# Joining a gated product to the seven block products of an output stage (Trainium2, one core)

## The chip, the cores and the metric

The kernel runs on one NeuronCore of one Trainium2 chip. The metric is device time in microseconds (us) of one execution. The kernel before takes 266.28 us (median of 4 runs, 266.19 to 266.54). PE is TensorE, PEld its weight loads, DVE is VectorE, ACT is ScalarE, POOL is GpSimd, SP the engine that issues the DMAs.

## The reference, cut to what matters

```python
xn = layernorm(x)                                    # x: 2048 x 640
# branch A: a diagonal complex recurrence over the 2048 steps, then the output map
h[t] = Lam_bar * h[t-1] + xn[t] @ B_bar.T            # 640 complex states
yA   = 2 * (h @ C.T).real + xn * Dskip               # re and im of h against re and im of C: K = 2 x 640
# branch B: a gated MLP with a mixing over time
z  = gelu(xn @ w_in)                                 # 2048 x 1728
g  = w_sp @ layernorm(z[:, 864:]) + b_sp[:, None]    # "spatial" product, 2048 x 2048 x 864
yB = (z[:, :864] * g) @ w_out                        # K = 864
out = x + yA + yB                                    # 2048 x 640
```

So the output is one sum over h (K = 1280, ten k-tiles of 128) and over the gated features (K = 864, six k-tiles of 128 and one of 96).

## The kernel before: what the change and the argument touch

The kernel lists all its operations with the data they read and write, and a scheduler of its own, with estimated durations, puts them in a fixed order on each engine. TensorE's order is the program's order. At run time each engine goes through its list in order and waits on semaphores. An operation that waits therefore holds up everything behind it on its engine.

The output is made in eight "pairs" of two row tiles. For each pair, a 2 x 2 x 2 block product of h and C is done with seven block products instead of eight (Winograd's form); each has five k-tiles. VectorE makes the sums that this form needs: those of C once (`ct_comb`), those of h for each pair (`h_comb`). The gated part is added without that form: four groups of seven k-tiles (`og`).

```python
# ... out_pair(j), cut: A, B are blocks, S, T are sums of blocks
prods = dict(P1=(A(0, 0), B(0, 0)), P2=(A(1, 0), B(1, 0)), P3=(S(3), B(1, 1)), P4=(A(1, 1), T(2)),
             P5=(S(0), B(0, 1)), P6=(S(1), T(0)), P7=(S(2), T(1)))
# prod: for q in range(5): e.matmul(ps[:, bk, c0:c1], lf(q), rf(q)[:, c0:c1], ...)    5 matmuls of 320 columns
# og:   for k in range(7): e.matmul(ps[:, bk, c0:c1], gv[0:kk, k, :], wov[0:kk, k, ...])  7 of them
X = bk()
prod("P1", X, True)
Z = bk()
cp(Z, X, "p1")                     # ScalarE copies PSUM bank X to Z; X goes on accumulating
while later:
    later.pop()()                  # the c22 group of the pair before
Q = bk()
prod("P5", Q, True)
add(fv(t12), Q, bv(0, 1), "t12"); add(fv(t22), Q, bv(1, 1), "t22")      # VectorE
prod("P6", X, False)               # must wait for the copy of X
V = bk()
cp(V, X, "u2")
prod("P2", Z, False);  og(0, 0, Z, False);  add(ov(0, 0), Z, bv(0, 0), "c11b")
prod("P7", X, False)
W = bk()                           # ... ScalarE copies X to W ("u3"); in the last pair in two parts, W and W2
prod("P3", V, False);  og(0, 1, V, False);  add(ov(0, 1), V, fv(t12), "c12b");  store(0)
prod("P4", X, False);  og(1, 0, X, False);  add(ov(1, 0), X, bv(1, 0), "c21b")
# finish(): og(1, 1, W), add "c22b", store(1): put off to the next pair; in the last pair done at once, in two parts
```

Before that comes the spatial stage, in the same form: eight rounds of seven products of eight k-tiles of 432 columns.

```python
prod(X, "A11", "B11", True, "P1")
ev(f(p1), X, b0, p1.iv(), "p1_%d" % j)               # ScalarE: PSUM to f32 in SBUF, with a bias
# ... P5, P6
prod(Z, "A12", "B21", True, "P2")
dve(tt(half(c0, 0), pb(Z), f(p1), ALU.add), ...)     # VectorE: c11 = P1 + P2
```

Two more parts matter. The "fixes" bring the recurrence's carried state into h: for each pair but the last, ScalarE scales it into one of four buffers `pq_m` (70 operations in all), and VectorE adds the buffer to h. And there are small VectorE operations on a few numbers per partition: 16 for powers of the eigenvalues, and the statistics of the second LayerNorm in four groups of four tiles.

## Time and profile before

| | before |
|---|---|
| time, median | 266.28 us |
| PE busy, matmuls | 258.7 us of a span of 263.9, 1517 |
| DVE busy | 238.8 us |
| ACT busy | 174.5 us |
| output stage, first matmul to last VectorE add | 69.12 us (192.44 to 261.56) |

The page's first part gives the busy time of each engine, its share of the span and its instructions:

```profile
PE 258.7 (98%) x1517; PEld 154.4 (58%) x1521; DVE 238.8 (91%) x574; ACT 174.5 (66%) x315; POOL 24.0 (9%) x41
```

Two engines look full. The chain that ended last says which one matters; its shares of the span by engine, then the costliest groups:

```profile
PE 95%; DMA 1%; SPq 1%; DVE 1%; issue 0%; POOL 0%
...
L994 PE MATMUL ps<-arena 128*128 128x432 bf16 x448 | 82.2, 346 | 0.0
...
L1113 PE MATMUL ps<-arena 128*128 128x320 bf16 x280 | 43.1, 299 | 0.0
```

L994 is the spatial stage, L1113 the h products; the gated groups are L1125. The 299 ns are one matmul from start to end; they overlap. What a matmul costs in a stream is read from the chain in order of time (start, us, what). This is one output period, from a P5 on (the first line is P5, P6 and P2); the last line is cut short by the end of the window:

```profile
201.86 2.04 PE ps L1113 x15
203.90 0.95 PE ps L1125 x7
204.85 1.36 PE ps L1113 x10
206.21 0.95 PE ps L1125 x7
207.16 0.68 PE ps L1113 x5
207.84 0.95 PE ps L1125 x7
208.79 0.68 PE ps L1113 x5
209.48 0.54 PE ps L1125 x4
```

Fifteen matmuls of 320 columns take 2.04 us, 0.136 each, and each piece begins where the one before ends: there is no gap. From the P1 of one pair to that of the next are 63 matmuls, 8.57 us. A change that takes matmuls away here should gain 0.136 us for each, as long as nothing else stops PE.

The first matmuls of the output stage and the end of the kernel, as timelines of PE and of VectorE in order of time (start, us, engine, line; idle time before and its releaser in brackets):

```profile
192.44 2.88 PE L1113 MATMUL ps<-arena 128*128 128x320 bf16 x20
...
258.45 0.84 PE L1113 MATMUL ps<-arena 128*128 128x320 bf16 x5
259.13 2.09 PE L1125 MATMUL ps<-arena 128*128 128x320 bf16 x21
...
260.28 0.49 DVE L1140 TENSOR_TENSOR arena<-ps,arena 128x320 bf16<-128x320 f32 x1 [1.14 <-PE ps L1125]
260.87 0.69 DVE L1187 TENSOR_TENSOR arena<-ps,arena 128x192 bf16<-128x192 f32 x2
```

The c21 add (260.28) runs while PE still does the 14 short matmuls of c22. The last add ends at 261.56, 0.34 us after PE.

### The profile page before, as it was taken

How to read it: one execution, taken by the hardware profiler on the slowest of the kernel's cores; microseconds unless marked ns; L12 is line 12 of the kernel's file. 1: busy time of each engine (PE TensorE's matmuls, PEld its weight loads, DVE VectorE, ACT ScalarE, POOL GpSimd, SP SyncE). 2: the span in 40 equal slices, each digit the busy share in tenths (PEclk: the TensorE clock that was granted, in tenths of full speed). 3: DMA queues.
4: the chain of work that ended last, by engine and by line, in shares of the span. 5: the costliest groups of instructions: out<-in, count | busy, mean ns of one | idle time of the engine just before them, and what ended most of it. 6: DMA issues, size and time to landing. Idle time of an engine off the chain costs nothing.

```text
span 263.9 us, 4352 instructions
## 1 busy us (share of the span) xinstructions
PE 258.7 (98%) x1517; PEld 154.4 (58%) x1521; DVE 238.8 (91%) x574; ACT 174.5 (66%) x315; POOL 24.0 (9%) x41
## 2 busy tenths in 40 slices
PE   7999999999999999999999999999999999999995
PEld 2555554444446777755555555555567777777774
DVE  4999999999999999999999999999999999965332
ACT  4899999989967454432223564689999999711110
POOL 4255076300000000000000000000000000000000
PEclk9999999999999999999999999999999999999999
DMA  6966999995002766498888978997245456675411
GB/s 201 361 83 125 195 221 197 301 234 104 0 0 58 202 186 170 125 234 154 213 201 156 225 139 192 192 250 225 52 137 142 113 126 156 147 214 132 99 52 50
DMA packets 88243, 41.98 MB, mean 159 GB/s; under 512 B 70974, under 2 KB 88222, under 8 KB 88222
## 3 DMA queue, kind: packets, MB, share of 16 engines
q1 hardware_dynamic: 88078, 41.66, 65.9%
q8 instruction: 12, 0.20, 0.3%
q14 instruction: 9, 0.07, 0.1%
q10 hardware_dynamic: 144, 0.05, 0.1%
HBM read 12.27 MB, written 12.45 MB: 94 GB/s over the span
## 4 chain that ended last, share of the span: by engine, by line
PE 95%; DMA 1%; SPq 1%; DVE 1%; issue 0%; POOL 0%
PE ps L994 31%; PE ps L596 19%; PE ps L679 16%; PE ps L1113 14%; PE ps L1125 12%; PE ps L617 2%; DMA arena<-in_A_x_dram 1%; SPq L370 1%; PE ps L560 0%; POOL arena L539 0%; DVE arena L544 0%; DVE arena L534 0%; DVE arena L1187 0%; DVE arena L537 0%; DVE arena L525 0%
## 5 line engine op out<-in xcount | busy, mean ns | idle before, releaser
L994 PE MATMUL ps<-arena 128*128 128x432 bf16 x448 | 82.2, 346 | 0.0
L994 PEld LDWEIGHTS ps<-arena 128*128 128x128 bf16 x448 | 43.7, 98 | 38.3 <-ACT arena L1007 0.8
L596 PE MATMUL ps<-arena 128*128 128x432 bf16 x280 | 51.6, 346 | 0.0
L786 ACT ACTIVATE arena<-arena 128x512 bf16<-128x512 bf16 x70 | 45.2, 712 | 1.7 <-DVE arena L751 1.4
L596 PEld LDWEIGHTS ps<-arena 128*128 128x128 bf16 x280 | 34.7, 124 | 16.1
L679 PE MATMUL ps<-arena 128*128 128x512 bf16 x196 | 43.0, 379 | 0.2
L1113 PE MATMUL ps<-arena 128*128 128x320 bf16 x280 | 43.1, 299 | 0.0
L1007 ACT ACTIVATE arena<-ps,arena 128x432 f32<-128x432 f32 (+1 forms) x32 | 19.6, 615 | 29.9 <-PE ps L994 29.9
L1125 PE MATMUL ps<-arena 128*128 128x320 bf16 (+3 forms) x231 | 35.6, 295 | 0.0
L1113 PEld LDWEIGHTS ps<-arena 128*128 128x128 bf16 x280 | 27.2, 97 | 11.0 <-ACT ps L1148 0.2
L679 PEld LDWEIGHTS ps<-arena 128*128 128x128 bf16 x200 | 19.6, 98 | 23.5 <-DMA arena<-in_A_B_im_dram 0.2
L1140 DVE TENSOR_TENSOR arena<-ps,arena 128x320 bf16<-128x320 f32 (+1 forms) x40 | 18.6, 484 | 12.5 <-PE ps L1125 11.9
L1125 PEld LDWEIGHTS ps<-arena 128*128 128x128 bf16 (+1 forms) x231 | 22.3, 98 | 8.3
L709 DVE SCALAR_TENSOR_TENSOR arena<-arena 128x512 f32<-128x512 bf16 x35 | 25.5, 744 | 0.0
L685 ACT CAST arena<-ps 128x512 bf16<-128x512 f32 x40 | 21.3, 601 | 4.4 <-PE ps L679 4.3
L790 DVE TENSOR_TENSOR arena<-arena 128x1024 bf16<-128x1024 bf16 (+1 forms) x42 | 23.6, 593 | 0.0
L665 ACT ACTIVATE arena<-ps 128x864 bf16<-128x864 f32 x16 | 14.3, 891 | 13.5 <-PE ps L596 13.4
L951 DVE TENSOR_TENSOR arena<-arena 128x1024 bf16<-128x1024 bf16 x32 | 21.3, 684 | 0.6 <-DMA arena<-in_B_w_sp_dram 0.6
L731 DVE TENSOR_TENSOR arena<-arena 128x512 f32<-128x512 f32 (+2 forms) x40 | 21.4, 550 | 0.0
L1148 ACT COPY ps<-ps 128x320 f32<-128x320 f32 x16 | 6.6, 412 | 16.6 <-PE ps L1113 16.6
L714 DVE SCALAR_TENSOR_TENSOR arena<-arena 128x256 bf16<-128x256 bf16 (+1 forms) x35 | 16.6, 477 | 0.0
L711 DVE SCALAR_TENSOR_TENSOR arena<-arena 128x256 bf16<-128x256 bf16 (+1 forms) x35 | 16.6, 475 | 0.0
(103 smaller groups left out, 259.4 us busy)
## 6 DMA issues: line engine op xcount, KB each, us to landing
g_scratch<-arena SPq DMA_DIRECT2D x16, 224.0 KB, 3.0
z_scratch<-arena SPq DMA_DIRECT2D x16, 216.0 KB, 2.5
arena<-z_scratch SPq DMA_DIRECT2D x8, 432.0 KB, 5.0
arena<-in_A_x_dram SPq DMA_DIRECT2D x16, 160.0 KB, 4.0
base_scratch<-arena SPq DMA_DIRECT2D x16, 160.0 KB, 2.2
arena<-base_scratch SPq DMA_DIRECT2D x16, 160.0 KB, 2.5
out_dram<-arena SPq DMA_DIRECT2D x15, 160.0 KB, 2.4
arena<-in_B_w_in_dram SPq DMA_DIRECT2D x6, 216.0 KB, 3.7
```

The lines of the kernel that those rows point to most:

```text
L596: r = e.matmul(ps[:, b + h, 0:FG], lhs(k), winv[:, k, hcol * FH + h * FG:hcol * FH + (h + 1) * FG], start=(k == 0), stop=(k == ND - 1))
L679: r = e.matmul(ps[:, b + ri, :], btv[:, ri, k, q * 128:(q + 1) * 128], xnTv[:, k, tq * 512:(tq + 1) * 512], start=(k == 0), stop=(k == ND ...
L685: act(lambda e, ri=ri: e.copy(o[:, ri, tq], ps[:, b + ri, :].rearrange("p (m j) -> p j m", j=8)), [bank(b + ri)], [l_m.iv((q * 8 + j) * 10 ...
L709: dve(lambda e: e.scalar_tensor_tensor(tv, prev, lr, cur, op0=ALU.mult, op1=ALU.add), pr + [l_iv(q, j)] + cr, [t.iv()], cd(512) + PTR, nm ...
L731: tt = lambda o, a, b, op: (lambda e: e.tensor_tensor(o, a, b, op))
L786: act(lambda e, pv=pv, hv=hv, lo=lo, sc=sc: e.activation(pv, hv[:, lo:lo + 2, 1:257], ACT.Identity, scale=sc), [h.iv(), Civ(cn)], [m.iv((q ...
L790: dve(lambda e, mv=mv, lq=lq: e.tensor_tensor(lq, lq, mv, ALU.add), li + [m.iv(0, 1024 * n)], li, cd(512 * n, 2), "fix%s%d%d" % (nm, q0, j))
L951: dve(lambda e: e.tensor_tensor(o.ap(1024), x.ap(1024), y.ap(1024), op), [x.iv(), y.iv()], [o.iv()], cd(1024, 2), "%s_%d" % (name, j))
L994: r = e.matmul(ps[:, bk, 0:FG], lv_[:, k, :], rv[k], start=(first and k == 0), stop=(k == 7), skip_group_check=True)
L1007: act(lambda e: e.activation(o, pb(bk), ACT.Identity, bias=bias), [bank(bk)] + bi, [dst], ca(FG, psum=True, ptr=1), name)
L1113: r = e.matmul(ps[:, bk, c0:c1], lf(q), rf(q)[:, c0:c1], start=(first and q == 0), stop=(q == 4), skip_group_check=True)
L1125: r = e.matmul(ps[:, bk, c0:c1], gv[0:kk, k, :], wov[0:kk, k, n * HD + c0:n * HD + c1], start=(first and k == 0), stop=(k == 6), skip_grou ...
```

## The change

Its intent: the gated product is another part of the same sum over K, so six of its k-tiles can join the block form: three k-tiles to each of the two K halves. Then the seven products have eight k-tiles each, and only the 96-row remainder is left for `og`. Four groups of six (24 matmuls) become seven groups of three (21): three fewer a pair. (In all it is 30 fewer and not 24, because the last c22 group was done in two parts, as 14 short matmuls, and is now 2; in columns it is 24 times 320.) VectorE must make the sums for the gated tiles too. To give it room, c11 is summed in PSUM: ScalarE copies P1 from one bank to another, PE adds P2 to it, and ScalarE evicts the sum with the bias. And the small VectorE operations become fewer.

```diff
-        pq_m = [q1.sub(2048) for _ in range(3)]          # and a fourth further down: four fix buffers
+        pq_m = [q2.sub(2048) for _ in range(3)]          # three
-        cb_m: 3 buffers, g_m: 4                           (cut)
+        cb_m: 2 buffers, g_m: 2, and wt_m: 3 for the sums of w_out
@@ small operations (cut)
-            for k in range(1, 9):                         # 16 operations on 5 numbers each
-                ... tensor_scalar(C("kr")[:, sl], C("dl")[:, 0:5], float(k), ...)
-                ... tensor_scalar(C("an")[:, ...], C("dl")[:, 5:10], float(k), ...)
+            pool(iota C("kv"))                            # then 2 operations on 40 numbers
+            dve(tensor_tensor(k3(C("kr")), k3(C("kv")), kb(C("dl")[:, 0:5]), ALU.mult))
+            dve(tensor_tensor(k3(C("an")[:, 40:80]), k3(C("kv")), kb(C("dl")[:, 5:10]), ALU.mult))
-            if i % 4 == 3:
-                z2_norm(i - 3, i + 1)
+            if i % 8 == 7:
+                z2_norm(i - 7, i + 1)
@@ c11
-            ev(f(p1), X, b0, p1.iv(), "p1_%d" % j)
+            act(lambda e: e.copy(pb(Z), pb(X)), [bank(X)], [bank(Z)], ...)
-            prod(Z, "A12", "B21", True, "P2")
-            dve(tt(half(c0, 0), pb(Z), f(p1), ALU.add), ...)
+            prod(Z, "A12", "B21", False, "P2")
+            ev(half(c0, 0), Z, b0, hiv(c0, 0), "c11_%d" % j)
@@ the join
+        def g_comb(j):                                    # four sums of 384 bf16 per pair, as in h_comb
+            ...
+            tt(S1, a21, a22, ALU.add, gi, i1, "GS1")
+            tt(S2, S1, a11, ALU.subtract, gi + [i1], i2, "GS2")
+            tt(S3, a11, a21, ALU.subtract, gi, i3, "GS3")
+            tt(S4, a12, S2, ALU.subtract, gi + [i2], i4, "GS4")
-                    for q in range(5):
+                    for q in range(8):                    # prod: k-tiles 5 to 7 are gated ones
-                    for k in range(7):                    # og
+                e.matmul(ps[:, bk, c0:c1], gvs[h][0:96, 6, :], wov[0:96, 6, ...], start=False, ...)   # og: one
-            while later:
-                later.pop()()
-                later.append(finish)
+                finish()                                  # c22 no longer put off
```

That a matmul may add to what ScalarE wrote rests on PSUM's accumulation. The Trainium skill, "PSUM — Partial Sum Buffer" (section "The four PSUM rules"), says that a matmul without the first-of-group flag adds to the old data where a matmul has written since the bank was last cleared by that flag, whoever wrote the data. The output stage used the same trick before.

More of the change, by code (lines that the diff above doesn't have):

```diff
@@ L298, in bass_parallel_sum__ssm_conv_s5__mixer_gmlp__prompt_kernel @@
         q1 = r1.again()
-        pq_m = [q1.sub(2048) for _ in range(3)]
+        wo_m = q1.sub(7 * 1280)
         cf_m = [q1.sub(1728) for _ in range(5)]
-        cb_m = [q1.sub(1728) for _ in range(3)]
+        cb_m = [q1.sub(1728) for _ in range(2)]
         z1i_m = [q1.sub(3456) for _ in range(2)]
-        g_m = [q1.sub(1792) for _ in range(4)]
+        g_m = [q1.sub(1792) for _ in range(2)]
         ct4_m = q1.sub(3200)
+        wt_m = [q1.sub(1920)]
         cp_m = Mem(r1.lo + 37760, 12800)
@@ L307, in bass_parallel_sum__ssm_conv_s5__mixer_gmlp__prompt_kernel @@
         q2 = r2.again()
-        wo_m = q2.sub(7 * 1280)
+        pq_m = [q2.sub(2048) for _ in range(3)]
         gT_m = [q2.sub(1792) for _ in range(4)]
         ct_m = [q2.sub(3200) for _ in range(2)] + [ct4_m]
-        pq_m.append(q2.sub(2048))
+        wt_m += [q2.sub(1920) for _ in range(2)]
         q3 = r3.again()
@@ L325, in bass_parallel_sum__ssm_conv_s5__mixer_gmlp__prompt_kernel @@
         prm_m = cst(128, BF16)
-        c_m = cst(440)
+        c_m = cst(512)
         st_m = cst(NT * 16)
@@ L409, in C @@
                 o = sum(c for _, c in cpos.values())
-                assert (o + n) <= 440
+                assert (o + n) <= 512
                 cpos[name] = (o, n)
@@ L476, in bass_parallel_sum__ssm_conv_s5__mixer_gmlp__prompt_kernel @@
              [ident_m.iv()], [ident_m.iv()], 0.3, "id1")
-        C("half", 4)
+        C("half", 8)
         C("e", 40)
@@ L634, in z2_norm @@
             if t0 < NHALF:
-                dve(lambda e: e.tensor_tensor(v(0), v(0), v(7), ALU.add), [vi(0), vi(7)], [vi(0)], 0.08, "z2s" + n)
+                h0, h7 = st2v[:, 0, t0:NHALF], st2v[:, 7, t0:NHALF]
+                dve(lambda e: e.tensor_tensor(h0, h0, h7, ALU.add), [s2iv(0, t0, NHALF), s2iv(7, t0, NHALF)],
+                    [s2iv(0, t0, NHALF)], 0.08, "z2s" + n)
             dve(lambda e: e.tensor_scalar(v(2), v(0), 1.0 / FH, None, op0=ALU.mult), [vi(0)], [vi(2)], 0.08, "z2m" + n)
@@ L814, in s5_consts @@
             C("an", 80)
-            for k in range(1, 9):
-                sl = slice((k - 1) * 5, k * 5)
-                dve(lambda e, k=k, sl=sl: e.tensor_scalar(C("kr")[:, sl], C("dl")[:, 0:5], float(k), None, op0=ALU.mult),
-                    [Civ("dl")], [Civ("kr")], 0.07, "kr%d" % k)
-                dve(lambda e, k=k, sl=sl: e.tensor_scalar(C("an")[:, 40 + (k - 1) * 5:40 + k * 5], C("dl")[:, 5:10],
-                                                          float(k), None, op0=ALU.mult),
-                    [Civ("dl")], [Civ("an")], 0.07, "an%d" % k)
+            C("kv", 40)
+            pool(lambda e: e.iota(C("kv"), pattern=[[1, 8], [0, 5]], base=1, channel_multiplier=0,
+                                  allow_small_or_imprecise_dtypes=True), [], [Civ("kv")], 0.2, "kv")
+            k3 = lambda a: a.rearrange("p (k q) -> p k q", k=8)
+            kb = lambda a: a.rearrange("p (o q) -> p o q", o=1).broadcast_to([128, 8, 5])
+            dve(lambda e: e.tensor_tensor(k3(C("kr")), k3(C("kv")), kb(C("dl")[:, 0:5]), ALU.mult), [Civ("dl"), Civ("kv")],
+                [Civ("kr")], 0.11, "kr")
+            dve(lambda e: e.tensor_tensor(k3(C("an")[:, 40:80]), k3(C("kv")), kb(C("dl")[:, 5:10]), ALU.mult),
+                [Civ("dl"), Civ("kv")], [Civ("an")], 0.11, "an")
             pool(lambda e: e.tensor_tensor(C("rk"), C("e"), C("kr"), ALU.pow), [Civ("kr"), Civ("e")], [Civ("rk")],
@@ L1008, in ev @@
                         ca(FG, psum=True, ptr=1), name)
-            p1, p5, u2, u3 = [ring(cf_m, ncf) for _ in range(4)]
+            p5, u2, u3 = [ring(cf_m, ncf) for _ in range(3)]
             f = lambda m: m.ap(FG, FP32)
@@ L1015, in spatial @@
             prod(X, "A11", "B11", True, "P1")
-            ev(f(p1), X, b0, p1.iv(), "p1_%d" % j)
+            act(lambda e: e.copy(pb(Z), pb(X)), [bank(X)], [bank(Z)], ca(FG, psum=True), "p1_%d" % j)
             prod(Y, "S1", "T1", True, "P5")
@@ L1020, in spatial @@
             ev(f(u2), X, b0, u2.iv(), "u2_%d" % j)
-            prod(Z, "A12", "B21", True, "P2")
-            dve(tt(half(c0, 0), pb(Z), f(p1), ALU.add), [bank(Z), p1.iv()], [hiv(c0, 0)], cd(FG), "c11_%d" % j)
+            prod(Z, "A12", "B21", False, "P2")
+            ev(half(c0, 0), Z, b0, hiv(c0, 0), "c11_%d" % j)
             prod(X, "S3", "T3", False, "P7")
@@ L1031, in spatial @@
             for h, c in ((0, c0), (1, c1)):
-                gm = g_m[ng[0] % 4]
-                gsem = ng[0] % 4
+                gm = g_m[ng[0] % 2]
                 ng[0] += 1
@@ L1041, in gate_st @@
             n = 2 * j + h
-            gsem = n % 4
+            gsem = n % 2
             dma("sp", g_d[n], gm.ap(896), [gm.iv()], [("gd", n, n + 1)], 128 * 1792, "gst%d%d" % (j, h), sem="gst%d" % gsem)
@@ L1058, in bass_parallel_sum__ssm_conv_s5__mixer_gmlp__prompt_kernel @@
         ctv = [m.ap(ND * HD).rearrange("p (q n) -> p q n", q=ND) for m in ct_m]
-        def ct_comb():
-            b11, b12 = cpv[:, 0, :, 0:HD], cpv[:, 0, :, HD:D]
-            b21, b22 = cpv[:, 1, :, 0:HD], cpv[:, 1, :, HD:D]
-            ci = [cp_m.iv()]
-            t2, t3, t4 = ctv
-            for o, x, y, w, name in ((t3, b22, b12, ct_m[1].iv(), "CT3"), (b12, b12, b11, cp_m.iv(0, 6400), "CT1"),
-                                     (t2, b22, b12, ct_m[0].iv(), "CT2"), (t4, b21, t2, ct_m[2].iv(), "CT4")):
-                dve(lambda e, o=o, x=x, y=y: e.tensor_tensor(o, x, y, ALU.subtract),
-                    ci + ([ct_m[0].iv()] if y is t2 else []), [w], cd(ND * HD, 2), name)
+        wtv = [m.ap(3 * HD).rearrange("p (k n) -> p k n", k=3) for m in wt_m]
@@ new lines, in b_sums @@
+        def b_sums(v, iv, n, tv, tm, name):
+            b11, b12, b21, b22 = v
+            t2, t3, t4 = tv
+            for o, x, y, w, nm in ((t3, b22, b12, tm[1].iv(), "3"), (b12, b12, b11, iv, "1"),
+                                   (t2, b22, b12, tm[0].iv(), "2"), (t4, b21, t2, tm[2].iv(), "4")):
+                dve(lambda e, o=o, x=x, y=y: e.tensor_tensor(o, x, y, ALU.subtract),
+                    [iv] + ([tm[0].iv()] if y is t2 else []), [w], cd(n, 2), name + nm)
+        def ct_comb():
+            b_sums([cpv[:, c, :, h * HD:(h + 1) * HD] for c in range(2) for h in range(2)], cp_m.iv(), ND * HD, ctv, ct_m,
+                   "CT")
@@ new lines, in wt_comb, with tt @@
+        def wt_comb():
+            b_sums([wov[:, c * 3:c * 3 + 3, h * HD:(h + 1) * HD] for c in range(2) for h in range(2)], wo_m.iv(0, 7680),
+                   3 * HD, wtv, wt_m, "WT")
+        def g_comb(j):
+            ms = hs_of[j]
+            ga, gb = gt_of[(j, 0)], gt_of[(j, 1)]
+            q = lambda m, c: m.ap(384, BF16, c * 768)
+            a11, a12, a21, a22 = q(ga, 0), q(ga, 1), q(gb, 0), q(gb, 1)
+            S1, S2, S3, S4 = [m.ap(384, BF16, 1280) for m in ms]
+            i1, i2, i3, i4 = [m.iv(1280, 768) for m in ms]
+            gi = [ga.iv(), gb.iv()]
+            def tt(o, x, y, op, r, w, name):
+                dve(lambda e: e.tensor_tensor(o, x, y, op), r, [w], cd(384, 2), "%s_%d" % (name, j))
+            tt(S1, a21, a22, ALU.add, gi, i1, "GS1")
+            tt(S2, S1, a11, ALU.subtract, gi + [i1], i2, "GS2")
+            tt(S3, a11, a21, ALU.subtract, gi, i3, "GS3")
+            tt(S4, a12, S2, ALU.subtract, gi + [i2], i4, "GS4")
@@ L1089, in bass_parallel_sum__ssm_conv_s5__mixer_gmlp__prompt_kernel @@
         nbk = [0]
-        later = []
         OUT_BANKS = (6, 7, 0, 1, 2, 3, 4, 5)
@@ L1100, in out_pair @@
             ms = hs_of[j]
-            S = lambda n: (lambda q, m=ms[n]: m.ap(128, BF16, q * 256), [ms[n].iv(0, 1280)])
-            A = lambda r, h: (lambda q: lj(q, j)[:, r * 256 + h * 128:r * 256 + h * 128 + 128], [l_iv(q, j) for q in range(5)])
-            B = lambda c, h: (lambda q: cpv[:, c, q, h * HD:(h + 1) * HD], [cp_m.iv()])
-            T = lambda n: (lambda q: ctv[n][:, q, :], [ct_m[n].iv()])
+            gts = [gt_of[(j, h)] for h in range(2)]
+            gvs = [m.ap(896).rearrange("p (k t) -> p k t", k=7) for m in gts]
+            S = lambda n: (lambda q, m=ms[n]: m.ap(128, BF16, q * 256), [ms[n].iv()])
+            A = lambda r, h: (lambda q: gvs[h][:, r * 3 + q - 5, :] if q > 4 else
+                              lj(q, j)[:, r * 256 + h * 128:r * 256 + h * 128 + 128], [l_iv(q, j) for q in range(5)] + [gts[h].iv()])
+            B = lambda c, h: (lambda q: (wov[:, c * 3 + q - 5] if q > 4 else cpv[:, c, q])[:, h * HD:(h + 1) * HD],
+                              [cp_m.iv(), wo_m.iv()])
+            T = lambda n: (lambda q: wtv[n][:, q - 5, :] if q > 4 else ctv[n][:, q, :], [ct_m[n].iv(), wt_m[n].iv()])
             prods = dict(P1=(A(0, 0), B(0, 0)), P2=(A(1, 0), B(1, 0)), P3=(S(3), B(1, 1)), P4=(A(1, 1), T(2)),
@@ L1111, in mm, with og @@
                 def mm(e):
-                    for q in range(5):
-                        r = e.matmul(ps[:, bk, c0:c1], lf(q), rf(q)[:, c0:c1], start=(first and q == 0), stop=(q == 4),
+                    for q in range(8):
+                        r = e.matmul(ps[:, bk, c0:c1], lf(q), rf(q)[:, c0:c1], start=(first and q == 0), stop=(q == 7),
                                      skip_group_check=True)
                     return r
-                pe(mm, lr + rr, [bank(bk)], 5 * ((c1 - c0) / 2350 - 0.0002), "h%s_%d" % (n, j))
-            def og(h, n, bk, first, c0=0, c1=HD):
-                gt = gt_of[(j, h)]
-                gv = gt.ap(896).rearrange("p (k t) -> p k t", k=7)
-                def mm(e):
-                    for k in range(7):
-                        kk = 128 if k < 6 else 96
-                        r = e.matmul(ps[:, bk, c0:c1], gv[0:kk, k, :], wov[0:kk, k, n * HD + c0:n * HD + c1],
-                                     start=(first and k == 0), stop=(k == 6), skip_group_check=True)
-                    return r
-                pe(mm, [gt.iv(), wo_m.iv()], [bank(bk)], 7 * ((c1 - c0) / 2350 - 0.0002), "og%d%d_%d" % (h, n, j))
+                pe(mm, lr + rr, [bank(bk)], 8 * ((c1 - c0) / 2350 - 0.0002), "h%s_%d" % (n, j))
+            def og(h, n, bk, c0=0, c1=HD):
+                pe(lambda e: e.matmul(ps[:, bk, c0:c1], gvs[h][0:96, 6, :], wov[0:96, 6, n * HD + c0:n * HD + c1],
+                                      start=False, stop=True, skip_group_check=True),
+                   [gts[h].iv(), wo_m.iv()], [bank(bk)], (c1 - c0) / 2350 + 0.002, "og%d%d_%d" % (h, n, j))
             t12, t22 = [ring(cf_m, ncf) for _ in range(2)]
@@ L1163, in out_pair @@
             prod("P2", Z, False)
-            og(0, 0, Z, False)
+            og(0, 0, Z)
             add(ov(0, 0), Z, bv(0, 0), "c11b")
@@ L1176, in out_pair @@
             prod("P3", V, False)
-            og(0, 1, V, False)
+            og(0, 1, V)
             add(ov(0, 1), V, fv(t12), "c12b")
@@ L1180, in out_pair @@
             prod("P4", X, False)
-            og(1, 0, X, False)
+            og(1, 0, X)
             add(ov(1, 0), X, bv(1, 0), "c21b")
@@ L1184, in finish @@
                 for q, w, c0, c1 in parts:
-                    og(1, 1, w, False, c0, c1)
+                    og(1, 1, w, c0, c1)
                     o = om[1].ap(HD, BF16, 640)
@@ L1217, in bass_parallel_sum__ssm_conv_s5__mixer_gmlp__prompt_kernel @@
             load_x(i + 11)
-        z2_norm(0, 4)
         ln_x(5)
@@ L1277, in next_out @@
             h_comb(j)
+            g_comb(j)
             out_pair(j, last=(j == 7))
-            no[0] = 2 * j
+            no[0] = 2 * j + 2
             pump()
@@ L1292, in bass_parallel_sum__ssm_conv_s5__mixer_gmlp__prompt_kernel @@
         load_wo()
+        wt_comb()
         for j in range(8):
```

## The prediction

> **What bounds the kernel now.** TensorE. Its matmuls are busy 258.7 of 263.9 us at granted clock 1.0 (page, parts 1 and 2), the chain that ended last is 95% PE, and from 9.3 us on PE waits for nothing but 0.9 us for an early LayerNorm (waits of PE). The pace is the streamed columns: in the chain a 320-column matmul costs 0.136 us (7 in 0.95 us), a 432-column one 0.183. The Trainium skill, "TensorE: Matmul & The Clock Gate" (section "Wait — 56ns, not 53.3ns?") gives N/2.4 GHz plus about 2.5 ns: 135.8 ns; the trace agrees. VectorE is 100% busy from 60 to 230 us (windows), but it runs ahead: the timeline shows h_comb of an output pair ending 3 us (pair 0) and 4 to 11 us (later pairs) before PE needs it. ScalarE is full from 178 to 229 us with the fixes, which end 6 to 13 us ahead of their pair.
>
> **What the change removes from PE.** An output pair has 7 products of 5 k-tiles and 4 gated groups of 7: 63 matmuls of 320 columns (8.57 us a pair in the chain). Afterwards: 7 x 8 plus 4 tails of one: 60. So 3 x 0.136 = 0.41 us a pair, 3.3 us over eight. The spatial stage keeps its 448 matmuls (82 us).
>
> The last pair gives some back: PE's split c22 groups (14 short matmuls, 0.99 us) covered VectorE's c21 add; as two matmuls they don't, so three adds (0.41 + 0.29 + 0.29 us spacing) follow PE in a row. Estimate: og10 ends 2.45 us earlier, the last add about 2.7 us earlier.
>
> **What it adds and moves, off PE.**
> - VectorE: g_comb, 4 adds of 384 bf16 a pair. From 0.40 us spacing at 640 and 0.60 at 1024, about 0.27 each: 8.5 us in all; four W sums 2.3 us. Gone: eight c11 adds (0.52 each, 4.1 us), 14 net coefficient operations and about 9 norm ones (roughly 0.08 spacing, 1.8 us). Net about +5 us, but before pair 0 about -1.5 us; afterwards 8.2 us of VectorE work a pair against 8.16 of PE until the fixes end. The lead survives.
> - ScalarE: c11 becomes an eviction (+0.5 us x 8), the p1 copy loses its bias (-0.1 x 8): +3 us, mostly where it has room. Fixes lose one of four buffers and may start up to 1 us later.
> - PSUM copies: the next product must wait for P1's copy; PE slack falls from 1.63 to 1.09 us (1.22 for u2, u3). Copies take 0.41 us and start up to 0.51 us late behind a fix: it just fits; I allow 0.2 us.
> - Gated tiles are needed at a pair's start, not near its end; their slots come free at the end of pair j for pair j+2. 3.3 us transpose plus 1.1 us sums against 8.16 us: fits.
>
> **Prediction.** 266.29 - 2.7 + 0.2 = 263.8 us; 8 in 10 between 263.0 and 265.4. Faster by over 2%: 0.01; within 2%: 0.96; slower by over 2%: 0.03.
>
> **What would show it.** PE matmuls 1517 -> about 1487, busy about 3 us less, pair period 8.57 -> 8.16 us, chain still about 95% PE, spatial stage ending near 192.6 us. VectorE busy +4 to +8 us while its full stretch still ends before about 242 us. At the end, about 1.1 us from the last matmul group to the last add instead of 0.3.
>
> **What would make it wrong.** PE waiting at pair starts on a transpose or g_comb; fixes starved by three buffers; stalls behind the PSUM copies at each pair; a rearranged static order that stops PE earlier.

## The result, and the profile after

| | before | after |
|---|---|---|
| time, median (range) | 266.28 us (266.19 to 266.54) | 263.88 us (263.51 to 264.02) |
| ratio | | 0.9906, 95% interval 0.9889 to 0.9923 |
| PE matmuls, busy | 1517, 258.7 us | 1487, 255.5 us |
| DVE busy, ACT busy | 238.8, 174.5 us | 242.3, 179.1 us |
| output stage | 69.12 us | 66.62 us |

A ratio is the mean time of one kernel's runs over that of the other's runs of the same rounds, so not quite the ratio of the medians. 263.8 was predicted and 263.88 measured: 0.9% faster, inside the 2% band and clear of noise. The outputs are right. The counts are those of the records: four are missing from both traces (other traces of kernels with as many matmuls have 1521 and 1491).

The page's first part, the chain by engine, and two groups of the changed kernel, where L1146 are the products, L1153 the remaining tails and L1094 the sums of the gated tiles:

```profile
PE 255.5 (98%) x1487; PEld 151.6 (58%) x1491; DVE 242.3 (93%) x579; ACT 179.1 (68%) x323; POOL 23.0 (9%) x38
...
PE 64%; DVE 18%; ACT 7%; DMA 6%; issue 3%; SPq 1%; POOL 1%; DVEq 0%
...
L1146 PE MATMUL ps<-arena 128*128 128x320 bf16 x448 | 64.6, 299 | 0.1
...
L1094 DVE TENSOR_TENSOR arena<-arena 128x384 bf16<-128x384 bf16 x32 | 10.9, 350 | 1.2 <-DMA arena<-g_scratch 0.9
```

One output pair in the chain in order of time, to set beside that of before:

```profile
201.54 4.35 PE ps L1146 x32
205.88 0.14 PE ps L1153
206.02 2.18 PE ps L1146 x16
208.20 0.14 PE ps L1153
208.34 1.09 PE ps L1146 x8
209.42 0.27 PE ps L1153 x2
```

There are 60 matmuls in 8.16 us, again 0.136 each and again without a gap: 0.41 us less a pair, as predicted. From pair 1's start (201.38 in PE's timeline) to pair 7's (250.35) are six such periods to the hundredth.

The same first matmuls and the end, in the timelines of PE and VectorE of the changed kernel:

```profile
192.90 4.82 PE L1146 MATMUL ps<-arena 128*128 128x320 bf16 x32
...
257.15 1.25 PE L1146 MATMUL ps<-arena 128*128 128x320 bf16 x8
258.24 0.44 PE L1153 MATMUL ps<-arena 96*128 96x320 bf16 x3
...
258.57 0.49 DVE L1167 TENSOR_TENSOR arena<-ps,arena 128x320 bf16<-128x320 f32 x1 [0.73 <-PE ps L1153]
258.98 0.54 DVE L1212 TENSOR_TENSOR arena<-ps,arena 128x192 bf16<-128x192 f32 x2
```

The tails after P4 are now three matmuls, and PE ends at 258.68, before the c21 add is half done. All three adds end after PE, the last 0.84 us after it, where before the last ended 0.34 after: 0.5 us given back. The prediction's sum had 0.6 (3.3 us saved, 2.7 left); the sign that it wrote down (1.1 instead of 0.3) would have been 0.8.

**What the chain says now, and what it doesn't.** PE's share of the chain fell from 95% to 64%, with 18% for VectorE. Read plainly, VectorE would now bound a good part of the kernel. But a chain is followed back through whatever released the last wait, however short that wait was. Here are the only waits of PE's weight loads in the output stage (engine, line, waited for: us, times, longest):

```profile
PEld ps L1146 <- ACT ps L1175: 0.5, 1, 0.5
```

One wait, at P6 of pair 0, for ScalarE's copy of P1. PE's matmuls lose about 0.3 us by it (pair 0 takes 192.90 to 201.38, 8.48 us, where later ones take 8.16). The walk back leaves PE there and goes mostly through ScalarE's and VectorE's queues for 53.6 us (195.37 back to 141.81), until it joins PE again. It leaves PE a second time at 38.80, where PE waited 0.3 us for a load, and doesn't come back to it for some 29 us. Two more profiles of this same kernel, taken for the experiments (e0 and e11), have PE at 91% and 89% of the chain:

```profile
PE 91%; DVE 2%; DMA 2%; ACT 2%; SPq 1%; issue 1%; DVEq 0%; POOL 0%
...
PE 89%; ACT 3%; DMA 3%; DVE 3%; SPq 1%; issue 1%; DVEq 0%
```

They have the same wait at P6 of pair 0 (0.4 us), but there the walk is back at PE after 10 and 15 us. Shares of the chain tell where the walk went, not what a faster VectorE would gain.

### The profile page after: what moved, and what is told of

Its sections match the earlier page's. It is cut to its first block, busy times and chain, and to the rows that moved or that the text cites. A ratio compares the mean times of both kernels' runs of the same rounds, so it can differ in the third digit from the quotient of the medians.

```text
span 261.9 us, 4305 instructions
## 1 busy us (share of the span) xinstructions
PE 255.5 (98%) x1487; PEld 151.6 (58%) x1491; DVE 242.3 (93%) x579; ACT 179.1 (68%) x323; POOL 23.0 (9%) x38
## 4 chain that ended last, share of the span: by engine, by line
PE 64%; DVE 18%; ACT 7%; DMA 6%; issue 3%; SPq 1%; POOL 1%; DVEq 0%
PE ps L1146 22%; PE ps L682 16%; PE ps L999 12%; PE ps L597 11%; DVE arena L956 3%; DMA arena<-in_A_B_im_dram 2%; DMA g_scratch<-arena 2%; ACT arena L789 2%; DVE arena L734 2%; DVE arena L1039 2%; PE ps L1153 2%; DMA arena<-in_A_x_dram 2%; DVE arena L579 1%; DVE arena L921 1%; DVE arena L919 1%
## 5 line engine op out<-in xcount | busy, mean ns | idle before, releaser
L999 PEld LDWEIGHTS ps<-arena 128*128 128x128 bf16 x448 | 43.7, 98 | 38.1 <-ACT arena L1012 0.4
L1146 PE MATMUL ps<-arena 128*128 128x320 bf16 x448 | 64.6, 299 | 0.1
L1146 PEld LDWEIGHTS ps<-arena 128*128 128x128 bf16 x448 | 43.5, 98 | 17.8 <-ACT ps L1175 0.5
L789 ACT ACTIVATE arena<-arena 128x512 bf16<-128x512 bf16 x70 | 45.8, 712 | 4.6 <-DVE arena L793 4.5
L597 PEld LDWEIGHTS ps<-arena 128*128 128x128 bf16 x280 | 34.7, 124 | 16.1
L682 PEld LDWEIGHTS ps<-arena 128*128 128x128 bf16 x200 | 19.5, 98 | 23.9 <-DMA arena<-in_A_B_im_dram 0.5
L793 DVE TENSOR_TENSOR arena<-arena 128x1024 bf16<-128x1024 bf16 (+1 forms) x42 | 23.8, 592 | 0.0
L1113 DVE TENSOR_TENSOR arena<-arena 128x640 bf16<-128x640 bf16 x32 | 15.2, 481 | 0.0
L1094 DVE TENSOR_TENSOR arena<-arena 128x384 bf16<-128x384 bf16 x32 | 10.9, 350 | 1.2 <-DMA arena<-g_scratch 0.9
```

Source lines behind the costliest of these rows:

```text
L597: r = e.matmul(ps[:, b + h, 0:FG], lhs(k), winv[:, k, hcol * FH + h * FG:hcol * FH + (h + 1) * FG], start=(k == 0), stop=(k == ND - 1))
L682: r = e.matmul(ps[:, b + ri, :], btv[:, ri, k, q * 128:(q + 1) * 128], xnTv[:, k, tq * 512:(tq + 1) * 512], start=(k == 0), stop=(k == ND ...
L789: act(lambda e, pv=pv, hv=hv, lo=lo, sc=sc: e.activation(pv, hv[:, lo:lo + 2, 1:257], ACT.Identity, scale=sc), [h.iv(), Civ(cn)], [m.iv((q ...
L793: dve(lambda e, mv=mv, lq=lq: e.tensor_tensor(lq, lq, mv, ALU.add), li + [m.iv(0, 1024 * n)], li, cd(512 * n, 2), "fix%s%d%d" % (nm, q0, j))
L999: r = e.matmul(ps[:, bk, 0:FG], lv_[:, k, :], rv[k], start=(first and k == 0), stop=(k == 7), skip_group_check=True)
L1146: r = e.matmul(ps[:, bk, c0:c1], lf(q), rf(q)[:, c0:c1], start=(first and q == 0), stop=(q == 7), skip_group_check=True)
```

## The experiments

Times are medians; each ratio is against the kernel before, on the same chip. Besides the time, one stage is compared from the traces: from the output stage's first matmul to the end of its last VectorE add. This is needed because the start of the kernel moves: in the 14 traces, the z1 stage (TensorE's products for the first half of z, just before the spatial stage) starts between 81.21 and 82.60 us, and this does not follow the version (the c11 variant, whose change comes after that point, starts it at 82.60; the kernel before at 81.21). In the ten traces of the changed kernel and of its variants e4 to e10, whose orders of instructions are the same up to there, it starts between 81.36 and 82.33.

| kernel | median us | ratio, 95% interval | output stage us | of it after PE's end |
|---|---|---|---|---|
| before | 266.28 | | 69.12 | 0.34 |
| after | 263.88 | 0.9906 (0.9889 to 0.9923) | 66.62 | 0.84 |
| e0_after | 264.24 | 0.9919 (0.9897 to 0.9940) | 66.59 | 0.84 |
| e11_after_again | 263.57 | 0.9897 (0.9875 to 0.9919) | 66.55 | 0.86 |
| e1_small_ops | 266.47 | 0.9999 (0.9982 to 1.0016) | 69.11 | 0.33 |
| e2_c11 | 266.20 | 0.9996 (0.9982 to 1.0010) | 69.32 | 0.34 |
| e3_join | 263.54 | 0.9903 (0.9883 to 0.9924) | 66.32 | 0.85 |
| e4_pad | 267.98 | 1.0063 (1.0039 to 1.0087) | 71.14 | 0.85 |
| e8_pad_same_order | 266.65 | 1.0012 (0.9988 to 1.0035) | 69.58 | 0.86 |
| e7_double_gsums | 267.38 | 1.0038 (1.0014 to 1.0062) | 70.24 | 0.85 |
| e5_tail | 263.41 | 0.9891 (0.9864 to 0.9917) | 66.31 | 0.53 |
| e6_four_fix_bufs | 263.39 | 0.9893 (0.9862 to 0.9924) | 66.34 | 0.85 |
| e9_tail_four_bufs | 262.55 | 0.9861 (0.9837 to 0.9885) | 66.09 | 0.53 |
| e10_split_c21 | 262.23 | 0.9856 (0.9827 to 0.9884) | 65.82 | 0.33 |

The theory (PE): the whole gain is 24 matmuls fewer. The rival (RELIEF): VectorE, full for 170 us and a quarter of the new chain with ScalarE, is a second limit, and taking operations off it is part of the gain.

### e0_after and e11_after_again: controls

The changed kernel without an edit.

> The changed kernel as it is, as a control on the chip of the next three. Every theory: 0.990 to 0.992 of before, 263.5 to 264.2 us. Its trace also says how much the start-up moves from run to run: in the first trace of the changed kernel the bu stage began 0.54 us later than before; if that is jitter of the first loads it will differ here, if it belongs to the change it will be 0.5 again.

> The changed kernel once more, as the control of this call: 0.990 to 0.992 of before; output stage 66.6 us with PE's wait of 0.3 us for pair 0's P1 copy.

They gave 264.24 and 263.57 us, 0.9919 and 0.9897 of before, each by a hair outside one of its stated ranges. The output stage repeats to 0.07 us (66.62, 66.59, 66.55); PE's loss at pair 0 is 0.30, 0.27 and 0.22 of it. The start of the bu stage (xn times B_bar, just before z1) did differ (39.16 in e0_after, where the first trace of the changed kernel had 38.80 and that of before 38.26), and variants with the same early order have it between 38.19 (e6) and 38.82 (e9), so the late start is no fixed part of the change. Medians of one kernel thus move by 0.7 us, and tenths are better read from the stage.

### e1_small_ops: the small operations alone

```diff
 kernel before, plus only:
-            16 operations for the powers; z2_norm in groups of four
+            iota and 2 operations; z2_norm in groups of eight
```

> The kernel before with only the small VectorE operations changed (powers of the eigenvalues by an iota and two products; z2 statistics in two groups of eight). Theory PE (TensorE's column count is the whole gain): 266.0 to 266.6 us, no change, since PE waits for none of these. Rival RELIEF (VectorE, full for 170 us, is a second limit, and taking operations off it is part of the gain): 265.3 to 265.8, 0.5 to 1 us faster.

266.47 us, ratio 0.9999; output stage 69.11. VectorE's busy time fell from 238.8 to 236.7 us, and nothing came of it. One operation on 5 numbers took 162 to 170 ns before; one on 40 numbers takes 192 to 196 ns. So the new form, two operations for sixteen, is the cheaper one. The Trainium skill, "VectorE: DVE Perf Modes" (section "Rules for kernel authors"), gives the same advice, to minimize the count of operations; the trace agrees. It gained no time because PE did not wait for VectorE.

### e2_c11: c11 in PSUM alone

```diff
 kernel before, plus only:
-            ev(f(p1), X, b0, ...);  prod(Z, "A12", "B21", True, "P2");  dve(c11 = P2 + p1)
+            act(copy Z <- X);       prod(Z, "A12", "B21", False, "P2"); ev(c11 <- Z, with the bias)
```

> The kernel before with only c11 moved: P1 copied within PSUM by ScalarE, P2 added to it by PE, evicted by ScalarE; 4 us less VectorE work, 3 us more ScalarE work, the same matmuls. Theory PE: 266.0 to 266.6 us. Rival RELIEF: 265.3 to 265.8.

266.20 us, ratio 0.9996. VectorE 3.2 us less busy, ScalarE 3.6 us more; the output stage is 69.32, 0.2 longer, with a wait of 0.4 us of the weight loads for ScalarE's copy of P1, at pair 0, by which PE's matmuls lose 0.19. The spatial stage, from its first matmul to that of the output stage, is 0.22 shorter (81.81 us for 82.03). RELIEF wanted 265.3 to 265.8 for each of these two and is rejected: neither gains.

### e3_join: the join alone

```diff
 kernel after, minus both:
-            p1 copied in PSUM, c11 evicted by ScalarE; the fewer small operations
+            p1 evicted with the bias, c11 added by VectorE; the 16 and the four groups as before
```

> The changed kernel with c11 and the small operations put back as before: the join alone, 24 matmuls fewer, but about 6 us more VectorE work than in the changed kernel, nearly all of it before output pair 0. Theory PE with the lead of several us that the prediction read: 263.8 to 264.4, all the gain. Rival ROOM (the two other parts gain nothing themselves, but make the room on VectorE that the join's sums need; the changed kernel's trace shows the sums of pairs 0 and 1 only about 3.5 us ahead of PE): 265 to 268, with PE idle 1 to 3 us around pairs 0 and 1 for h_comb, g_comb or the fixes.

263.54 us, ratio 0.9903: all of the gain, and 0.26 us under the stated range. The output stage, 66.32, is even 0.3 shorter than in the changed kernel, for pair 0's wait is not there. But the spatial stage is 82.24 us, with two waits of PE's weight loads for ScalarE, against 81.76 to 81.95 in three traces of the changed kernel. Both stages together are 148.56 us here and 148.57, 148.35 and 148.31 there (151.15 in the kernel before). ROOM, the idea that the other two parts make the place that the sums need, falls as well. VectorE is busy for 248.0 us (94%) here, and the last sum of a pair comes up to 1.8 us after that pair's P5 starts. But P5 needs only the first sum; P3, which needs the fourth, starts 4.5 us after P5 (33 matmuls of 0.136). PE never waits for VectorE in the output stage. So neither of the two other parts showed a gain in time, alone or as a help to the join; by the two stages, in these traces, they are worth 0.25 us at most.

### e4_pad and e8_pad_same_order: three matmuls put back

```diff
 kernel after (e4: as an operation of its own, which the scheduler sees)
+            pe(pad, ...)      # three 320-column matmuls into P5's bank, which P5 then starts anew
 kernel after (e8: inside P5's operation, not told to the scheduler)
+                    for q in range(3 if n == "P5" else 0):
+                        e.matmul(ps[:, bk, c0:c1], lf(q), rf(q)[:, c0:c1], start=(q == 0), stop=(q == 2), ...)
                     for q in range(8):
```

> The changed kernel with three idle 320-column matmuls put back into each output pair (written to the bank that P5 then starts anew, so the result is right): as many matmuls as before. Theory PE: 24 x 0.136 = 3.3 us more than the changed kernel, about 267.1, a little slower than before, for the changed order at the end costs 0.5 us and start-up some tenths. Rival RELIEF: only part of it comes back, 265 to 266.3.

267.98 us; the output stage 71.14, 4.5 us longer than in the changed kernel (66.62) and not 3.3. The result is right in both kernels. The excess is a new wait. It can be followed in the timelines of PE, VectorE and ScalarE around pair 3:

```profile
223.60 0.90 DVE L1094 TENSOR_TENSOR arena<-arena 128x384 bf16<-128x384 bf16 x3 [1.03 <-DMA arena<-g_scratch]
...
225.14 1.95 ACT L789 ACTIVATE arena<-arena 128x512 bf16<-128x512 bf16 x3 [1.70 <-DVE arena L793]
...
226.99 0.41 ACT L1206 COPY ps<-ps 128x320 f32<-128x320 f32 x1
...
227.46 1.26 PE L1146 MATMUL ps<-arena 128*128 128x320 bf16 x8 [1.10 <-ACT ps L1206]
```

In the rearranged order VectorE waits 1.03 us for a transposed gated tile; the fix add behind it (L793) is late; ScalarE's next fixes (L789) wait 1.70 us for the buffer that this add frees; the u3 copy stands behind them; and P4 waits 1.10 us for it. P4 should start at 226.20, when the tail before it has had its 0.136 us, and starts at 227.46: 1.26 us. The 24 matmuls make 3.26, together 4.52, as measured. (The wait of 0.30 us at P6 of pair 0 is gone, and one of 0.29 us elsewhere in pair 0 stands in its place.) This run tests two things at once, so it was done again with the order left as it was.

> The changed kernel with three more 320-column matmuls at the head of every P5 (into a bank that P5 then starts anew), added without telling the kernel's own scheduler, so that the order of instructions on every other engine stays that of the changed kernel. In e4_pad the padding came to 4.5 us in the output stage, of which 1.26 us was one wait for ScalarE's u3 copy in pair 3, after a rearranged order. Theory PE: 24 x 0.136 = 3.3 us in the output stage, at most 0.3 us of other waits, and 267.0 to 267.6 us in all. If 4.5 us come again, the matmuls cost more than their columns.

266.65 us, ratio 1.0012: the gain is gone, 3.1 us slower than the changed kernel (263.57). The output stage is 69.58, from the first to the end of the last of these:

```profile
192.65 1.25 PE L1149 MATMUL ps<-arena 128*128 128x320 bf16 x8
...
261.68 0.55 DVE L1215 TENSOR_TENSOR arena<-ps,arena 128x192 bf16<-128x192 f32 x2
```

ScalarE's and VectorE's instructions are in the order of the changed kernel. The wait at pair 0 is not there, since P5's three extra matmuls give ScalarE's copy 0.41 us more. Against the two kernels that have the join without that wait (66.32 and 66.34) this is 3.25 us, for 24 x 0.136 = 3.26; against the control (66.55, with a loss of 0.22 us at pair 0) it is 3.25 too. And PE's part of the stage is 68.72 us, where the kernel before, with as many columns, has 68.78. So the columns are the gain; it comes back to 0.01 us. The time came out 0.35 us under the stated range, since I had counted on starting from the stage of the changed kernel with its wait.

### e7_double_gsums: how much room VectorE has

```diff
 kernel after
             tt(S4, a12, S2, ALU.subtract, gi + [i2], i4, "GS4")
+            tt(S1, ...); tt(S2, ...); tt(S3, ...); tt(S4, ...)      # the four sums once more
```

> The changed kernel with g_comb's four sums done twice in each pair: 8.5 us more VectorE work, 1.07 us a pair, no PE work. If VectorE's lead at the output is as the prediction read it (4 to 11 us, growing): same as the changed kernel within 0.3 us. If it is about 3 us and no longer grows, as the changed kernel's trace suggests: PE stands at the pair starts from pair 2 to 4 on, 2 to 5 us slower, 266 to 269.

267.38 us, output stage 3.6 us longer than in the changed kernel. The longest waits in the output stage, of PE's weight loads and of its matmuls:

```profile
PEld ps L1150 <- DVE arena L1094: 3.7, 5, 1.4
...
PE ps L1150 <- DVE arena L1094: 2.1, 3, 1.1
```

The three of the matmuls fall at pairs 6 and 7 (PE's timeline has them at 244.7, 247.1 and 255.0), not from pair 2 to 4 on as expected. Probably 1.07 us a pair takes that long to use up what VectorE is ahead. The scheduler saw the new sums, and the order on VectorE and ScalarE changed, and the weight loads also wait 1.5 us for ScalarE's copies; so how much of the 3.6 us is VectorE's work alone is not shown. There is room, but not much. Here is the time from the last sum of a pair to the start of its P5, read from the timelines (sums end at, P5 starts at):

```
pair        0     1     2     3     4     5     6     7
before    2.9   5.3   6.7   7.5   8.6  10.5  12.0  12.1    us ahead, grows
after     4.5   4.2   4.1   3.4   3.2   3.2   2.1   3.4    flat or shrinking
e3_join   1.4  -0.1  -0.2  -0.8  -0.8  -0.8  -1.8   0.1    and PE still doesn't wait (P3 is 4.5 us later)
```

The prediction's reading that "the lead survives" holds for the change and is a matter of a few us: some 6 us of VectorE work more, nearly all of it ahead of pair 0 (e3), cost nothing in the output stage; 8.1 us more (busy), spread over the pairs, with the new order (e7), cost 3.6.

### e5_tail: the end

```diff
 kernel after, last pair only
+            finish()                     # c22: W has all it needs after P7
             prod("P4", X, False);  og(1, 0, X);  add(ov(1, 0), X, bv(1, 0), "c21b")
-            finish()
```

> The changed kernel with the last pair's c22 group, which doesn't need P4, put ahead of P4: same matmuls. Theory TAIL (the end gives back 0.5 us because three adds follow PE's last matmul in a row): two of the three adds go under P4; from PE's end to the last add about 0.5 instead of 0.84 us, and PE's end itself unchanged, so 0.5 us (0.3 to 0.7) faster than the changed kernel: 263.2 to 263.6. If the end were set by the stores instead: no change.

263.41 us. The output stage fell by 0.31 us, to 66.31, for PE's end to the last add is 0.53 instead of 0.84 us. VectorE at the end:

```profile
257.95 0.54 DVE L1209 TENSOR_TENSOR arena<-ps,arena 128x192 bf16<-128x192 f32 x2
258.91 0.49 DVE L1167 TENSOR_TENSOR arena<-ps,arena 128x320 bf16<-128x320 f32 x1 [0.41 <-PE ps L1153]
```

Two adds now run under P4. TAIL is shown in the stage, at the low end of what I expected: I had written 0.5 us, though the difference of 0.84 and 0.5 in the same sentence is 0.34.

### e6_four_fix_bufs: the wait at pair 0

```diff
 kernel after
-        cf_m = [q1.sub(1728) for _ in range(5)]
+        cf_m = [q1.sub(1728) for _ in range(4)];  pq4_m = q1.sub(2048)      # fourth fix buffer
```

> The changed kernel with four fix buffers as before (room taken from one of five f32 eviction buffers). Theory BUF (three buffers make ScalarE wait for VectorE, 4.5 us of waits in the changed kernel against 0.3 before, which delays the copy of pair 0's P1 and stops PE by 0.3 us): waits under 1 us, PE's stall gone, 0.3 us faster, 263.5 to 263.7. Else (the stall comes of the ScalarE order around pair 0): 263.8 to 264.0, stall still there.

263.39 us, just under the stated range; output stage 66.34, 0.28 less, and PE's matmuls wait for nothing in it. ScalarE's waits for VectorE's fix adds, in the changed kernel and here:

```profile
ACT arena L789 <- DVE arena L793: 4.5, 6, 1.8
```

```profile
ACT arena L790 <- DVE arena L794: 1.4, 3, 0.9
```

How ScalarE's lateness stops PE is seen in the changed kernel's timeline of ScalarE before pair 0 and PE's weight load after it:

```profile
190.14 0.72 ACT L789 ACTIVATE arena<-arena 128x512 bf16<-128x512 bf16 x1 [1.84 <-DVE arena L793]
...
194.90 0.42 ACT L1175 COPY ps<-ps 128x320 f32<-128x320 f32 x1
...
195.37 2.02 PEld L1146 LDWEIGHTS ps<-arena 128*128 128x128 bf16 x16 [0.47 <-ACT ps L1175]
```

ScalarE idles 1.84 us for a buffer to come free; everything behind is late; and the copy of P1, which could begin at 194.0, when P1's eight matmuls are done, begins at 194.90, behind an eviction and a fix. P5 covers 1.09 us of that. (The 1.63 us that the prediction gives for before hold for the later pairs; pair 0 has no put-off c22 group, so P5 alone covered 0.68 us there, and the copy was just in time.)

So a fourth buffer takes the wait away, as BUF expected, but three buffers alone don't make it. e3 has three as well, ScalarE waits for them as long, and its copy of P1 is still in time:

```profile
ACT arena L787 <- DVE arena L791: 4.9, 7, 1.8
...
194.31 1.34 ACT L787 ACTIVATE arena<-arena 128x512 bf16<-128x512 bf16 x2 [1.83 <-DVE arena L791]
...
195.55 0.41 ACT L1171 COPY ps<-ps 128x320 f32<-128x320 f32 x1
```

There PE loses nothing at pair 0, while e2, with four buffers and c11 in PSUM, loses 0.19 us. The wait thus comes of how much ScalarE has in its queue before the copy, to which the buffers, c11 and the scheduler's order may each add. e6 also got another order from about 140 us on, so their shares stay open. In e6 1.4 us of ScalarE's waits stay, where under 1 was expected.

### e9_tail_four_bufs and e10_split_c21: a version that beats both

e9 is e5 and e6 together. e10 also splits the last P4 into 192 and 128 columns in two banks, so that the last add is a short one.

```diff
 e9, last pair only
-                prod("P4", X, False);  og(1, 0, X);  add(ov(1, 0), X, bv(1, 0), "c21b")
+                prod("P4", X, False, 0, 192);  og(1, 0, X, 0, 192);  add(..., "c21b", 0, 192);  store(1, "act", 0, 192)
+                prod("P4", X2, False, 192, HD);  og(1, 0, X2, 192, HD);  add(..., "c21b2", 192, HD);  store(1, "sp", 192, HD)
+                # X2: a copy of X's columns 192 to 320 after P7, made by ScalarE
```

> The changed kernel with e5's order of the last pair and e6's fourth fix buffer together. Both theories (TAIL and BUF) add: in the output stage 66.6 - 0.3 - 0.3 = 66.0 us from its first matmul to the last add; 0.5 to 0.8 us faster than the changed kernel of the same call, 263.0 to 263.5 us.

> e9 with the last pair's P4 split into 192 and 128 columns in two banks, so that the last add is of 128 elements instead of 320: from PE's end to the last add 0.3 instead of 0.5 us, PE itself some hundredths longer: 65.85 us for the output stage, 0.1 to 0.2 us faster than e9 at best, hard to tell in the time.

262.55 and 262.23 us, against 263.57 for the changed kernel; output stages 66.09 and 65.82 against 66.55. What the traces show is 0.73 us for e10, of which e9 has 0.46. The medians differ by 1.34; the rest is probably the start of the kernel, where these edits leave the order of instructions as it was: e10's trace has its z1 stage 0.84 us earlier than the control's. That is one trace of each, and doesn't show it for the medians. e9's time is below its stated range, and its 1.02 us above the 0.5 to 0.8 expected; in the stage e9 expected 66.0 and e10 65.85, so the parts add. (PE loses 0.09 us at pair 0 in e9's trace and nothing in e10's.) Both gave the right result. e10's chain is PE to the end once more:

```profile
PE 96%; DVE 1%; DMA 1%; issue 0%; POOL 0%; SPq 0%
```

## Why the prediction was right

- **What bounds the kernel: right.** PE, at 0.136 us for 320 columns. The matmuls put back in the same order (e8) took the gain away to 0.01 us (3.25 us for 3.26). The trace's count of matmuls fell from 1517 to 1487, as predicted.
- **The pair period, 8.57 to 8.16 us: right** to the hundredth.
- **The end gives back some of it: right in kind.** Three adds end after PE, the last 0.84 us after it instead of 0.34: 0.5 us, near the 0.6 of the prediction's sum and less than its sign of 1.1 instead of 0.3. e5 took 0.31 of the 0.5 back by moving one group.
- **The sum.** The output stage was to become about 2.7 us shorter but for 0.2 us of waits. Without its wait it is 2.80 shorter (69.12 to 66.32 in e3), and the wait came to 0.3: 2.5 us in the stage, 2.4 in the medians. That the medians meet the sum to 0.1 us is partly luck: in the two calls with a control the same change gave 2.30 and 2.75. The wait was named (PSUM copies behind ScalarE's fixes), but reckoned from a slack that shrinks in every pair; it came at pair 0 alone, where the slack grew (0.68 to 1.09 us) and the copy began 0.9 us late. The three buffers were named as a risk; a fourth takes the wait away (e6), yet three don't make it by themselves (e3).
- **No gain from the VectorE parts: right,** and shown separately (e1, e2 and e3). The prediction was thin on why the change has them. As a help to the join they aren't needed (e3).
- **The lead of VectorE: right in kind, too generous in outlook.** It shrank from as much as 12 us to between 2.2 and 4.5 and no longer grows. e7 shows where it ends.
- **Three more readings announced for the profile did not come out.** "Chain still about 95% PE" was 64%, by two waits of half a microsecond and less (and 91% and 89% in other traces of the same kernel). VectorE's busy time rose by 3.5 us, not by 4 to 8; the runs split it: the join adds 9.2 us (e3), where 10.8 were reckoned, the small operations take off 2.1 (e1) and c11 takes off 3.2 (e2), where 1.8 and 4.1 were; that makes 3.9, near the 3.5. And its full stretch ends near 246 us, not before 242 (the first longer idle time in its timeline is 0.86 us before 246.79). None of these carried the predicted time.

What stays open: what the buffers, c11 and the order each have in the wait at pair 0; and why the first traces of one kernel and another differ by up to 1.4 us before the z1 stage. The waits there are for the first loads and for what hangs on them, and no run was made on it. So the gains of e9 and e10 are claimed only as far as the stage shows them.

## What to carry to other kernels

Where the chain is one engine without gaps, count that engine's work: a saved matmul is worth its columns, and an operation saved on another engine, however full, was worth nothing here while the leading engine didn't wait for it. Before you trust a share of the chain, look up the wait at which the chain leaves the leading engine: here two waits of 0.5 and 0.3 us turned a third of the chain over to engines that cost nothing. And when a change takes buffers for itself, look at who loses them: here a fourth buffer with the order that came with it, one group put ahead of another at the end, and a split last product brought 0.73 us more in the stage, on the 2.5 of the change.

## What the Trainium skill lacked or had wrong

- "TensorE: Matmul & The Clock Gate", section "Back-to-back issue gap", says that in a stream of weight loads and matmuls the spacing is about 81 ns at 128 columns and about 131 ns at 512, and that N/2.4 GHz plus 2.5 ns holds for single matmuls only. These runs show the plain formula in long streams with a weight load for each matmul: 0.136 us at 320 columns (15 in 2.04 us), 0.183 at 432 (448 in 82.03) and 0.216 at 512 (200 in 43.17, e0_after); at 128 columns, in e10's end, 8 in 0.45 us, so 56 ns. The section "Wait — 56ns, not 53.3ns?" of the same page has it right.
- "PSUM — Partial Sum Buffer", section "Specifications (TRN2)", has ScalarE writes faster to PSUM than to SBUF. For a copy of 128 x 432 f32 from PSUM the changed kernel shows no difference: 508 ns to PSUM and 511 ns to SBUF, eight of each. (The bias costs: 615 ns.)
- "Perfetto Trace Analysis", section "Identifying the Most-Contended Engine", takes the engine of highest occupancy for the one to work on, and judges TensorE by MFU (the share of its peak rate) and by the busy share of its weight loads instead. That share was 58%, so by it VectorE, 91% busy and full for 170 us, would come first; taking 2.1 or 3.2 us off VectorE (e1, e2) changed nothing. MFU was not worked out here, and may point to TensorE.
- No page that I read says how far the share of the chain moves with one short wait: 64%, 91% and 89% for PE in three traces of one kernel.
- No page that I read gives the scatter of the time up to a stage some 80 us into a kernel: the z1 stage began between 81.21 and 82.60 us in 14 traces, while the output stage of one kernel repeated to 0.07 us.
